# Start-up loads, early stores and the next-memory copy of a recurrent attention kernel re-planned together

## The chip, the cores and the metric

The kernel runs on one core of a Trainium2 chip. The metric is the device time of one execution in microseconds (us), taken over several runs; the profile shows one execution and its span, which is some 1.8 us shorter than the time of the same run. The engines are PE (TensorE, matmuls; "PEld" are its weight loads), DVE (VectorE), ACT (ScalarE), POOL (GpSimd) and SP (SyncE, which only issues transfers).

## The reference

Two layers of recurrent attention with a small memory, each followed by a dense layer, every one on the layernorm of its input and added to it:

```python
for s in range(n_seg):                       # 2048 rows in 64 segments of 32, one after the other
    h = concatenate([mem, x[s]])             # 8 rows of memory + 32 rows, 512 columns
    q, k, v = h @ Wq, h @ Wk, h @ Wv         # 32 heads of 128
    p = softmax(where(mask, q @ k.T * scale, -1e9))
    o = (p @ v) @ Wo                         # back to 512 columns
    mem = o[:8]                              # the next segment needs it
    out.append(o[8:])
...
x = x + A(layernorm(x)); x = x + B(layernorm(x))     # B: 512 -> 1376 -> relu -> 512
x = x + A(layernorm(x)); x = x + B(layernorm(x))     # the same weights again
```

The memory chains the 64 segments. What a segment needs of `x` alone (values, layernorm) can be done ahead; what it needs of `mem` can't.

## The kernel before

The two attention layers are interleaved, the second one four segments behind, which gives 68 steps (0 to 67). The kernel does not write its instructions in a fixed order. It first describes all operations to a planner, each with its engine, its estimated cost and the keys that it reads and writes; the planner simulates the engines, picks by priority among the operations that are ready, and the operations are then issued in the planned order. The priorities are tables of numbers found by search, one entry for a kind of operation and a phase of the run (step 0 and step 2 have a phase each, steps 1 and 3 share one, the even and the odd middle steps have one each, and so have the even and the odd last steps):

```python
RULE = (0.0714, 334.5336, ...)      # look-ahead, bonus for staying in the column mode, ...
PERIOD = 40.244
PLACE = {("attend.mmu0.0", 0): 609.348, ("attend.mmu0.0", 1): -183.486, ... }   # PE operations
PAIRED = { ... }                    # matmul groups that may be cut into 64-column halves
AHEAD = { ... }                     # operations of the other engines

            if PE in o.cost:
                o.prio = PERIOD * o.step + PLACE.get((o.key, phase(o.step)), 0.0)
            ...
                # a rule of the planner's model, not a measurement: a block of 64 matmuls
                # is planned to end no sooner than FETCH us after the block four before it
                for i in range(issued // BLOCK + 1, (issued + n) // BLOCK + 1):
                    t1 += max(0.0, blocks[-4] + FETCH - (t1 + ...))
```

The parts that the change touches:

```python
    # prepare(): the first loads, on ACT's queue
        plan.op(ACT, 0.45, get_x, w=[xb0])             # x rows of group 0
        plan.op(ACT, 0.45, get_memory, w=[mb0])
    ...
    # prepare_group(g): x rows of groups 1 to 7, also on ACT's queue
            plan.op(*((ACT, 0.45) if early else (SP, 0.78)), load, r=[*gate, *(rows if g > 1 else [])], ...)
    ...
    # project(k): once the output of step k is in the PSUM bank st, its memory rows go to HT,
    # which the queries and keys of step k+1 read
            def ev():
                nc.vector.tensor_copy(out=HTn[:, :, m_lo:m_hi], in_=v(2 * W)[:, :, m_lo:m_hi])

            plan.op(DVE, 0.15, ev, r=[wo], w=[("HTm", i), ("taken", k)])
    ...
    # main loop: POOL writes the early groups' x and values back to HBM (early_stores), SP then loads
    # the dense weights into the room that those values held (load_dense)
            if k in (1, 2):
                while stores:
                    early_stores([("sc", 1, 0)])       # behind the first scores of step 1
                load_dense(k, u)
```

Of the kernel before, what the change touches and what calls it, by code (L numbers as in the profile page):

```python
# [28 lines left out]
BLOCK, FETCH = 64, 7.0  # L29

RULE = (0.0714, 334.5336, 21842.5159, 2217302446.7678)
PERIOD = 40.244
PLACE = {
    ("attend.mmu0.0", 0): 609.348, ("attend.mmu0.0", 1): -183.486, ("attend.mmu0.0", 2): 147.437,
    ("attend.mmu0.0", 3): -78.515, ("attend.mmu0.0", 4): 65.61, ("attend.mmu0.0", 5): 366.858,
    ("attend.mmu0.0", 6): -249.718, ("attend.mmu1.0", 0): 726.903, ("attend.mmu1.0", 1): 684.118,
    ("attend.mmu1.0", 2): -19.8, ("attend.mmu1.0", 3): 132.658, ("attend.mmu1.0", 4): 129.759,
    ("attend.mmu1.0", 5): 371.411, ("attend.mmu1.0", 6): -353.4, ("attend.mmu2.0", 0): -14.873,
    ("attend.mmu2.0", 1): -1055.665, ("attend.mmu2.0", 2): 375.184, ("attend.mmu2.0", 3): 495.749,
    ("attend.mmu2.0", 4): 267.365, ("attend.mmu2.0", 5): 143.496, ("attend.mmu2.0", 6): -164.881,  # L40
    ("attend.mmu3.0", 0): 55.83, ("attend.mmu3.0", 1): 304.958, ("attend.mmu3.0", 2): -27.575,
    ("attend.mmu3.0", 3): 521.565, ("attend.mmu3.0", 4): -53.654, ("attend.mmu3.0", 5): -33.75,
    ("attend.mmu3.0", 6): 139.713, ("attend.mmu4.0", 0): -1004.936, ("attend.mmu4.0", 1): -1157.418,
    ("attend.mmu4.0", 2): -270.186, ("attend.mmu4.0", 3): -964.038, ("attend.mmu4.0", 4): -328.51,
    ("attend.mmu4.0", 5): 58.406, ("attend.mmu4.0", 6): -138.434, ("dense_layer.mm.0", 1): 844.726,
    ("dense_layer.mm.0", 3): 771.51, ("dense_layer.mm.0", 6): 794.222, ("dense_layer.mm.1", 1): 595.059,
    ("dense_layer.mm.1", 3): 282.976, ("dense_layer.mm.1", 6): -365.611, ("dense_layer.mm.2", 1): 402.759,
    ("dense_layer.mm.2", 3): 201.475, ("dense_layer.mm.2", 6): 383.89, ("dense_layer.mm.3", 1): 375.463,
    ("dense_layer.mm.3", 3): 375.816, ("dense_layer.mm.3", 6): 544.49, ("dense_layer.mm.4", 1): -1179.846,
    ("dense_layer.mm.4", 3): -271.405, ("dense_layer.mm.4", 6): -220.579, ("dense_layer.mm.5", 1): 907.374,  # L50
    ("dense_layer.mm.5", 3): 373.845, ("dense_layer.mm.5", 6): 565.451, ("finish_pair.turn.0", 1): -90.833,
    ("finish_pair.turn.0", 3): -375.688, ("finish_pair.turn.0", 6): -738.706, ("g0", 2): -581.803,
    ("g1", 2): -1043.701, ("g2", 2): 282.751, ("g3", 2): -205.545, ("g4", 2): 584.676, ("g5", 2): -60.649,
    ("g6", 2): 371.668, ("g7", 2): 288.938, ("late_values.mmv0.0", 0): -64.904, ("late_values.mmv1.0", 0): 678.294,
    ("late_values.mmv2.0", 0): 101.482, ("late_values.mmv3.0", 0): 44.512, ("late_values.mmv4.0", 0): 351.071,
    ("late_values.mmv5.0", 0): -24.294, ("late_values.mmv6.0", 0): -120.477, ("late_values.mmv7.0", 0): -996.402,
    ("layernorm.turn.0", 1): 92.873, ("layernorm.turn.0", 3): -23.204, ("layernorm.turn.0", 6): 193.698,
    ("layernorm.turn.1", 1): 910.291, ("layernorm.turn.1", 3): -857.558, ("layernorm.turnr.0", 0): -337.322,
    ("layernorm.turnr.1", 0): -831.277, ("prepare.turns.0", 2): 390.358, ("project.mm.0", 0): 359.615,
    ("project.mm.0", 1): -869.571, ("project.mm.0", 2): -60.568, ("project.mm.0", 3): -169.635,  # L60
    ("project.mm.0", 4): 156.569, ("project.mm.0", 5): 430.997, ("project.mm.0", 6): -293.953,
    ("project.mm.1", 0): 824.231, ("project.mm.1", 1): 252.725, ("project.mm.1", 2): 43.429,
    ("project.mm.1", 3): 540.792, ("project.mm.1", 4): -164.609, ("project.mm.1", 5): 588.5,
    ("project.mm.1", 6): 101.76, ("project.mm.2", 0): 126.782, ("project.mm.2", 1): -862.581,
    ("project.mm.2", 2): -235.851, ("project.mm.2", 3): 70.544, ("project.mm.2", 4): -259.138,
    ("project.mm.2", 5): -117.671, ("project.mm.2", 6): -300.67, ("project.mm.3", 0): 223.614,
    ("project.mm.3", 1): -213.188, ("project.mm.3", 2): -93.552, ("project.mm.3", 3): 545.141,
    ("project.mm.3", 4): 351.716, ("project.mm.3", 5): -238.608, ("project.mm.3", 6): -107.853,
    ("project.mm.4", 0): 230.883, ("project.mm.4", 1): -148.91, ("project.mm.4", 2): -568.124,
    ("project.mm.4", 3): 379.873, ("project.mm.4", 4): -132.884, ("project.mm.4", 5): 770.552,  # L70
    ("project.mm.4", 6): 66.643, ("queries_keys.mmu0.0", 0): -119.1, ("queries_keys.mmu0.0", 1): -850.808,
    ("queries_keys.mmu0.0", 2): -204.722, ("queries_keys.mmu0.0", 3): -113.926, ("queries_keys.mmu0.0", 4): 59.817,
    ("queries_keys.mmu0.0", 5): -235.287, ("queries_keys.mmu0.0", 6): -320.902,
    ("queries_keys.mmu0.1", 0): -402.058, ("queries_keys.mmu0.1", 1): 10.017, ("queries_keys.mmu0.1", 2): 261.017,
    ("queries_keys.mmu0.1", 3): -213.134, ("queries_keys.mmu0.1", 4): -297.361, ("queries_keys.mmu0.1", 5): -84.629,
    ("queries_keys.mmu0.1", 6): -888.993, ("queries_keys.mmu0.2", 0): -392.541,
    ("queries_keys.mmu0.2", 1): -333.397, ("queries_keys.mmu0.2", 2): -356.282, ("queries_keys.mmu0.2", 3): -51.387,
    ("queries_keys.mmu0.2", 4): -331.518, ("queries_keys.mmu0.2", 5): -853.492,
    ("queries_keys.mmu0.2", 6): -1044.343, ("queries_keys.mmu0.3", 0): -40.65, ("queries_keys.mmu0.3", 1): -57.543,
    ("queries_keys.mmu0.3", 2): -41.34, ("queries_keys.mmu0.3", 3): -1060.763, ("queries_keys.mmu0.3", 4): -376.858,  # L80
    ("queries_keys.mmu0.3", 5): -120.052, ("queries_keys.mmu0.3", 6): -111.195,
    ("queries_keys.mmu1.0", 0): -259.357, ("queries_keys.mmu1.0", 1): -373.272, ("queries_keys.mmu1.0", 2): 371.489,
    ("queries_keys.mmu1.0", 3): -1015.198, ("queries_keys.mmu1.0", 4): 169.449,
    ("queries_keys.mmu1.0", 5): -376.609, ("queries_keys.mmu1.0", 6): -35.359, ("queries_keys.mmu1.1", 0): -890.304,
    ("queries_keys.mmu1.1", 1): -52.862, ("queries_keys.mmu1.1", 2): 261.214, ("queries_keys.mmu1.1", 3): -931.873,
    ("queries_keys.mmu1.1", 4): -80.004, ("queries_keys.mmu1.1", 5): -905.415, ("queries_keys.mmu1.1", 6): -75.569,
    ("queries_keys.mmu1.2", 0): -1032.537, ("queries_keys.mmu1.2", 1): -941.562,
    ("queries_keys.mmu1.2", 2): -245.647, ("queries_keys.mmu1.2", 3): -738.459, ("queries_keys.mmu1.2", 4): 282.479,
    ("queries_keys.mmu1.2", 5): -47.448, ("queries_keys.mmu1.2", 6): -355.274, ("queries_keys.mmu1.3", 0): -1042.76,
    ("queries_keys.mmu1.3", 1): -311.787, ("queries_keys.mmu1.3", 2): -329.768,  # L90
    ("queries_keys.mmu1.3", 3): -856.085, ("queries_keys.mmu1.3", 4): -47.655, ("queries_keys.mmu1.3", 5): -394.586,
    ("queries_keys.mmu1.3", 6): -257.527, ("queries_keys.mmu2.0", 0): -51.901, ("queries_keys.mmu2.0", 1): -283.405,
    ("queries_keys.mmu2.0", 2): -257.559, ("queries_keys.mmu2.0", 3): 302.184, ("queries_keys.mmu2.0", 4): 98.406,
    ("queries_keys.mmu2.0", 5): 305.605, ("queries_keys.mmu2.0", 6): 363.104, ("queries_keys.mmu2.1", 0): -34.459,
    ("queries_keys.mmu2.1", 1): 44.98, ("queries_keys.mmu2.1", 2): 334.384, ("queries_keys.mmu2.1", 3): -1093.708,
    ("queries_keys.mmu2.1", 4): -293.392, ("queries_keys.mmu2.1", 5): 351.704,
    ("queries_keys.mmu2.1", 6): -1178.673, ("queries_keys.mmu2.2", 0): -41.303, ("queries_keys.mmu2.2", 1): 58.94,
    ("queries_keys.mmu2.2", 2): 291.775, ("queries_keys.mmu2.2", 3): 52.266, ("queries_keys.mmu2.2", 4): -151.786,
    ("queries_keys.mmu2.2", 5): 228.689, ("queries_keys.mmu2.2", 6): 405.936, ("queries_keys.mmu2.3", 0): 330.979,
    ("queries_keys.mmu2.3", 1): 57.914, ("queries_keys.mmu2.3", 2): -40.37, ("queries_keys.mmu2.3", 3): 87.416,  # L100
# [1234 lines left out]
```

## Time and profile before

| | before |
|---|---|
| time, median (lowest to highest) | 1631.96 us (1631.00 to 1634.06), 4 runs beside the changed kernel; 1632.44, 3 runs, known at the prediction |
| span of the profiled run | 1630.9 us |
| PE, ACT, DVE busy | 97%, 66%, 64% |
| PE matmuls, priced at the trace's issue spacing | 1531.8 us |
| first Wv matmul | 12.72 us |
| next-memory copy of step 0, 4, 64, 66 | 56.64, 138.28, 1564.35, 1600.04 us |
| middle steps, even and odd (medians of steps 5 to 63) | 25.33, 22.15 us |

### The profile page before, as it was taken

The page shows a single profiled execution, that of the slowest core. Times are in us where ns is not written, and L with a number is a line of the kernel's source. Part 1 is how long each engine was busy: PE and PEld are TensorE (multiplying, and loading weights), DVE is VectorE, ACT ScalarE, POOL GpSimd, SP SyncE. Part 2 cuts the span into 40 slices and gives each one's busy share as a digit, 9 for nine tenths or more (in the row PEclk, how much of TensorE's full clock was granted, in tenths as well). Part 3 has the DMA queues.
Part 4 walks back from the last instruction along what each step waited for, and adds up shares of the span by engine and source line. Part 5 has one row for each costly group of instructions (what it writes and reads, how often), then busy time and mean ns, then how long its engine had stood idle before and what let it go on. Part 6 is the DMA issues. An engine that isn't in the chain of part 4 may idle for free.

```text
span 1630.9 us, 94544 instructions
## 1 busy us (share of the span) xinstructions
PE 1587.0 (97%) x43116; PEld 1380.4 (85%) x43179; DVE 1046.2 (64%) x3025; ACT 1079.6 (66%) x2717; POOL 139.9 (9%) x363
## 2 busy tenths in 40 slices
PE   7999999999999999999999999999999999999997
PEld 4778888888888888888888888888888888888886
DVE  4556766766665666676567567656656765665664
ACT  4556766766666676666667666666766666676664
POOL 4210000001000000100000010000000000000000
PEclk9999999999999999999999999999999999999999
DMA  9521001111100111111011011101101000000000
GB/s 370 199 85 36 18 23 27 25 26 35 34 21 22 29 25 25 35 29 25 23 29 25 25 35 28 25 23 29 25 26 26 25 19 19 19 20 19 16 6 6
DMA packets 42880, 63.30 MB, mean 39 GB/s; under 512 B 15400, under 2 KB 28816, under 8 KB 42480
## 3 DMA queue, kind: packets, MB, share of 16 engines
q1 hardware_dynamic: 35984, 35.88, 9.0%
q0 software_dynamic: 5328, 20.32, 3.3%
q8 instruction: 338, 5.54, 1.4%
q10 hardware_dynamic: 1168, 1.06, 0.2%
q14 instruction: 62, 0.51, 0.1%
HBM read 33.50 MB, written 11.93 MB: 28 GB/s over the span
## 4 chain that ended last, share of the span: by engine, by line
PE 93%; DVE 4%; issue 1%; ACT 1%; DMA 0%; POOL 0%; DVEq 0%; POOLq 0%; ACTq 0%
PE work L667 38%; PE st L667 19%; PE fill L1000 16%; PE fill L667 12%; PE work L1168 4%; PE work L1084 3%; DVE sm L1109 1%; DVE es L1095 1%; DVE mx L1099 1%; DVE P L1126 0%; DVE HT L1212 0%; DVE es L1102 0%; PE fill L791 0%; DMA xb<-in_A_x_dram 0%; ACT OT L921 0%
## 5 line engine op out<-in xcount | busy, mean ns | idle before, releaser
L667 PE MATMUL work<-HT,Wk_sb 128*128 128x80 bf16 (+2 forms) x10144 | 363.6, 200 | 9.7 <-DVE HT L1212 9.2
L667 PE MATMUL work<-HT,Wq_sb 128*128 128x80 bf16 (+2 forms) x9728 | 361.5, 200 | 0.4 <-DVE HT L1212 0.2
L667 PEld LDWEIGHTS <-Wk_sb 128*128 128x128 bf16 (+1 forms) x10144 | 330.8, 103 | 29.7 <-DVE HT L1212 12.8
L667 PE MATMUL st<-OT,Wo_sb 128*128 128x80 bf16 (+1 forms) x8704 | 339.7, 199 | 3.8 <-issue 1.8
L667 PEld LDWEIGHTS <-Wq_sb 128*128 128x128 bf16 (+1 forms) x9728 | 326.9, 102 | 13.5 <-DVE HT L1212 5.1
L667 PEld LDWEIGHTS <-Wo_sb 128*128 128x128 bf16 x8704 | 319.2, 99 | 13.1 <-issue 6.1
L1000 PE MATMUL fill<-Wv_sb,HT 128*64 128x512 bf16 x2176 | 273.5, 382 | 0.0
L921 ACT CAST kT<-work 128x320 bf16<-128x320 f32 (+1 forms) x537 | 219.8, 410 | 71.4 <-PE work L667 35.3
L921 ACT CAST qT<-work 128x320 bf16<-128x320 f32 (+1 forms) x484 | 197.8, 409 | 102.5 <-PE work L667 58.4
L1149 ACT ACTIVATE PT<-work,half 128x160 bf16<-128x160 f32 (+2 forms) x447 | 203.0, 469 | 18.0 <-DVE PT L1151 14.0
L921 ACT CAST OT<-work 128x320 bf16<-128x320 f32 (+1 forms) x387 | 149.6, 415 | 98.0 <-PE work L1168 97.9
L921 ACT CAST vw<-fill 128x512 bf16<-128x512 f32 x229 | 134.2, 586 | 104.2 <-PE fill L1000 102.1
L1095 DVE TENSOR_TENSOR es<-work,maskb 128x320 f32<-128x320 f32 (+2 forms) x340 | 130.5, 400 | 84.4 <-PE work L1084 81.6
L1000 PEld LDWEIGHTS <-HT 128*64 128x64 bf16 x2176 | 107.2, 110 | 72.5 <-issue 1.9
L1106 ACT ACTIVATE es<-es 128x320 f32<-128x320 f32 (+2 forms) x340 | 133.2, 406 | 8.3 <-DVE es L1102 3.5
L1126 DVE TENSOR_TENSOR P<-es,sm 128x320 bf16<-128x320 f32 (+2 forms) x337 | 131.2, 406 | 4.4
L1151 DVE TENSOR_SCALAR PT<-work,half 128x320 bf16<-128x320 f32 (+2 forms) x233 | 105.0, 454 | 44.8 <-PE work L667 42.7
L1102 DVE TENSOR_TENSOR es<-es,mx 128x320 f32<-128x320 f32 (+2 forms) x340 | 131.5, 403 | 1.5
L1099 DVE TENSOR_REDUCE mx<-es 128x8 f32<-128x320 f32 (+2 forms) x340 | 129.5, 397 | 2.8
L1109 DVE TENSOR_REDUCE sm<-es 128x8 f32<-128x320 f32 (+2 forms) x340 | 128.5, 394 | 1.6 <-ACT es L1106 1.5
L1212 DVE CAST HT<-st 128x64 bf16<-128x64 f32 (+1 forms) x67 | 14.8, 221 | 163.3 <-PE st L667 163.0
L1168 PE MATMUL work<-PT,vw 128*64 128x80 bf16 (+1 forms) x1384 | 106.1, 202 | 1.8 <-DVE PT L1151 1.7
(99 smaller groups left out, 1729.6 us busy)
## 6 DMA issues: line engine op xcount, KB each, us to landing
V<-vw SPq DMA_DIRECT2D x240, 48.0 KB
V<-vh SPq DMA_DIRECT2D x120, 64.0 KB
Wq_sb<-in_A_Wq_dram POOLq DMA_DIRECT2D x2, 2048.0 KB, 20.7
Wk_sb<-in_A_Wk_dram POOLq DMA_DIRECT2D x2, 2048.0 KB, 25.0
Wo_sb<-in_A_Wo_dram POOLq DMA_DIRECT2D x2, 2048.0 KB, 36.1
vh<-vg SPq DMA_DIRECT2D x32, 128.0 KB
Wv_sb<-in_A_Wv_dram POOLq DMA_DIRECT2D x1, 2048.0 KB, 12.1
vh<-w_sb POOLq DMA_DIRECT2D x4, 512.0 KB, 7.2
```

The lines of the kernel that those rows point to most:

```text
L667: nc.tensor.matmul(out_[u:v, :], lhsT=lhsT[:, u:v], rhs=rhs, start=start, stop=stop, tile_position=(0, u), **more)
L921: nc.scalar.copy(out=out_, in_=in_)
L1000: nc.tensor.matmul(vp[64 * b:64 * b + 64, :], lhsT=cols(c4), rhs=Wv_sb[:, c4, n * 512:(n + 1) * 512], start=(c4 == 0), stop=(c4 == NC4 - 1 ...
L1095: nc.vector.tensor_tensor(out=flat(es[:, A]), in0=flat(sp[:, A]), op=ALU.add, in1=maskb[:, a_lo:a_hi, :].unsqueeze(2).to_broadcast([128, n ...
L1099: nc.vector.tensor_reduce(out=mx[:, As], in_=es3(), axis=AX.X, op=ALU.max)
L1102: nc.vector.tensor_tensor(out=es3(), in0=es3(), op=ALU.subtract, in1=mx[:, As].unsqueeze(2).to_broadcast([128, ns * na, L]))
L1106: nc.scalar.activation(out=es[:, A], in_=es[:, A], func=ACTF.Exp, scale=SCALE)
L1109: nc.vector.tensor_reduce(out=sm[:, As], in_=es3(), axis=AX.X, op=ALU.add)
L1126: (nc.gpsimd if eng == POOL else nc.vector).tensor_tensor(out=o, in0=flat(es[:, A]), op=ALU.mult, in1=sm[:, As].rearrange("p (a s) -> p a ...
L1149: nc.scalar.activation(out=o, in_=i, func=ACTF.Copy, scale=half[:, b:b + 1])
L1151: nc.vector.tensor_scalar_mul(out=o, in0=i, scalar1=half[:, b:b + 1])
L1168: nc.tensor.matmul(o[u:u + cols, :, a, :], lhsT=V[:, p, e0 + u:e0 + u + cols], rhs=PT[:, a, 2 * i + h2, :, :], start=True, stop=True, tile ...
```

## The change

The intent: PE is starved at the start, so bring x of group 0 in first, get the early stores and dense weights out of the way right behind the last attention weights, let whichever engine is free copy the next memory, and find the priorities again for the new plan. The hunks that are not tables:

```diff
-BLOCK, FETCH = 64, 7.0
+BLOCK, FETCH, LOADED = 64, 7.0, (75.0, 9.5)        # 9.5 in place of FETCH up to 75 us of planned time
-RULE = (0.0714, 334.5336, 21842.5159, 2217302446.7678)
-PERIOD = 40.244
+RULE = (0.0676, 338.0438, 3554579.0286, 1242705613.0663)
+PERIOD = 42.8582
 ... PLACE, PAIRED, AHEAD: every number new ...
-                    t1 += max(0.0, blocks[-4] + FETCH - (...))
+                    t1 += max(0.0, blocks[-4] + (FETCH if t > LOADED[0] else LOADED[1]) - (...))

-        plan.op(ACT, 0.45, get_x, w=[xb0])
-        plan.op(ACT, 0.45, get_memory, w=[mb0])
+        plan.op(ACT, 0.45, get_x, w=[xb0, "x0"])
+        plan.op(ACT, 0.45, get_memory, r=["x0"], w=[mb0, "start"])
 ...
-  ... load, r=[*gate, *(rows if g > 1 else [])],
+  ... load, r=[*gate, *(["start"] if early else []), *(rows if g > 1 else [])],

-            def ev():
-                nc.vector.tensor_copy(out=HTn[:, :, m_lo:m_hi], in_=v(2 * W)[:, :, m_lo:m_hi])
-            plan.op(DVE, 0.15, ev, r=[wo], w=[("HTm", i), ("taken", k)])
+            def ev(eng):
+                copy_on(eng, HTn[:, :, m_lo:m_hi], v(2 * W)[:, :, m_lo:m_hi])
+            copy_op(64, ev, r=[wo], w=[("HTm", i), ("taken", k)], more={ACT: 0.01, DVE: 0.02})

             if k in (1, 2):
-                while stores:
-                    early_stores([("sc", 1, 0)])
                 load_dense(k, u)
 ...
         project(k, act, seg)
+        while stores:
+            early_stores([("taken", 0)])               # behind the next-memory copy of step 0
```

## The prediction

> **What bounds the kernel now.** I read the page first, then the busy time by stretch, then the timeline of TensorE (PE) at both ends and in one middle step, then its waits.
>
> ```profile
> PE 1587.0 (97%) x43116; PEld 1380.4 (85%) x43179; DVE 1046.2 (64%) x3025; ACT 1079.6 (66%) x2717; POOL 139.9 (9%) x363
> PEclk9999999999999999999999999999999999999999
> q8 instruction: 338, 5.54, 1.4%
> ```
>
> PE is busy 97% of 1630.9 us at full granted clock; no other engine passes 66%. So the change can only win PE's idle 44 us, or make PE do less. The stretches say where the idle time lies (columns: us; busy and instructions of PE, PEld, DVE, ACT, POOL; clock, DMA share, GB/s):
>
> ```profile
> 0.00:40.00 40.00, 27.86 (x374) 17.17 (x375) 17.14 (x47) 19.60 (x39) 15.81 (x39) 1.00 0.96 370
> 40.00:80.00 40.00, 39.09 (x1044) 30.19 (x1041) 22.22 (x86) 23.61 (x73) 11.00 (x23) 1.00 0.56 200
> 80.00:120.00 40.00, 36.81 (x1040) 30.91 (x1036) 24.04 (x91) 23.98 (x78) 5.84 (x15) 1.00 0.32 96
> 600.00:900.00 300.00, 297.34 (x8106) 260.92 (x8117) 200.23 (x564) 205.48 (x506) 22.43 (x60) 1.00 0.11 27
> 1600.00:1631.00 31.00, 21.66 (x561) 17.94 (x560) 14.06 (x51) 11.88 (x38) 0.79 (x2) 0.87 0.03 7
> ```
>
> Idle are 12.1 us in the first 40, 3.2 us in 80 to 120, 2.7 us in a middle stretch of 300, and 9.3 us in the last 31. The tail (layernorm, dense layer and store of the last rows) is a chain that the change does not touch. What it aims at is the first 120 us. PE's own timeline there:
>
> ```profile
> 9.29 0.61 PE L667 MATMUL fill<-ident,xr 128*128 128x128 bf16 x4 [2.01 <-DVE xr L718]
> 11.44 0.61 PE L667 MATMUL fill<-ident,xr 128*128 128x128 bf16 x4 [1.54 <-DVE xr L718]
> 12.72 3.63 PE L1000 MATMUL fill<-Wv_sb,xg 128*64 128x512 bf16 x16 [0.68 <-ACT xg L921]
> ...
> 44.12 0.73 PE L667 MATMUL work<-HT,Wk_sb 128*128 128x40 bf16 x23 [0.47 <-issue]
> ...
> 89.58 0.20 PE L667 MATMUL st<-OT,Wo_sb 128*128 128x40 bf16 x2 [1.41 <-issue]
> ```
>
> PE starts real work at 12.72 us. "<-issue" means that nothing the profile shows held it. I counted PE's instructions in program order: the six such pauses (44.12, 50.86, 82.84, 89.58, 93.59, 97.59 us) come before instructions 960, 1216, 3008, 3264, 3520, 3776, all 192 past a multiple of 256. So PE waits for its next block of instructions; they sum to 2.9 us. Where DMA is nearly full (0.97 to 1.03 busy at 40 to 50 and 80 to 90 us) two such pauses end 6.74 us apart; at 90 to 100 (0.08) 4.0 us apart.
>
> [...] the first 16 Wv matmuls take 213 ns each (12.72 to 16.13), later ones 108; but it lasts until 19 us. The granted clock row doesn't show it. [...] the trace issues 16 in 0.574 us, 35.9 each. [...] 338 packets x 256 = 86,528 against 86,360 PE instructions[...] VectorE (DVE) sits idle 163 us ahead of the 64 next-memory copies.
>
> **The change part by part.** The instruction orders of both programs were compared; most of the diff is priorities for the order, found again.
>
> Amount of work. Counted by shape and priced at this trace's issue spacing (35.9 ns for 128x80, 18 for its 64-column half, 108 for 64x512, and so on), PE's matmuls sum to 1531.8 us before and 1531.9 after. The 567 extra matmuls are whole ones cut in halves (Wq: 480 fewer of 35.9 ns, 960 more of 18): 0 us. Switches between 64- and 128-column mode cost about 0.09 us (812.42 to 812.52); 309 become 303: -0.5 us (eight fewer in the last three steps, two more at the start).
>
> x of group 0 first. Now the order on ScalarE's (ACT's) queue is group 1, group 0, memory, and x0 lands 5.6 us after issue (1.25 to 6.87). Group 0 will be issued at 0.79 and group 1 about 1 us later than now. DVE can't begin on x0 before 5.2 us (it fills banks until 5.19). From there by this trace's durations: statistics 0.7 and 0.2, power 0.9, normalise 0.4, transpose 0.6: group 0 turned at about 8.0 instead of 9.9. But the new PE order still puts group 1's transpose ahead of the first Wv matmul. Its power now queues behind three weight issues of 0.8 on GpSimd (7.0 + 2.4 + 0.8 = 10.2), normalise and transpose 1.1: 11.3 to 11.4 us against 12.72. **-1.3 us**.
>
> Early stores and dense weights. Today GpSimd stalls 12.7 us (54.3 to 67.0) and the stores and dense weights use DMA at 70 to 90 us, with 1.77 us of PE idle in 80 to 90. DMA is free at 60 to 70 (0.01 busy). The 7 stores of 640 KB and 2.8 MB of weights, 7.3 MB, at some 380 GB/s take 19 us: they move to about 50 to 70. That removes the 89.58 and 82.84 pauses, and some of the waits behind. Steps 1 to 4, by the spacing of their next-memory copies (17.9, 19.9, 18.5, 25.4 us) less their matmul work (16.9, 15.8, 15.7, 23.1), lose 10.1 us; 8 mode switches each (0.7) and 0.3 of handover would be 4. Of the 6 us excess I give 3 back: **-3 us**. Against it: PE wants a block of 256 every 4.6 us in 50 to 70 (526 matmuls in 20 us)[...]. Some pauses move there: **+1 us**, and part of the early start may be eaten at instruction 960 in the same way.
>
> Next memory on either engine. All 67 copies go from DVE to ACT. A DVE copy of 128x64 takes 225 ns; ACT takes 266 for 128 columns and 292 for 160, so about 215 for 64 (an estimate). The matmuls that fit between the last st matmul and the first that needs the copy are the same in the steady steps (649 ns in one step, none in the next), so 36 steps stay exposed: 36 x 10 ns, **-0.4 us**.
>
> Middle. Matmul work between step ends is identical step by step (24.44 and 21.43 us). The last 7 odd two-sided steps lose 1.5 us each against 0.7 before them, to softmax and OT waits; the new order starts scores there sooner. I give **-1 us**.
>
> Sum: -0.5 -1.3 -3 +1 -0.4 -1 = -5.2 us, so 1632.4 becomes about 1627.
>
> **Rivals.** (1) *Instruction fetch becomes the startup's limit.* For: the pauses at 44.12 and 50.86 already sit at full DMA, and the change keeps DMA full until 70. At 6.7 us a block, four blocks take 27 us instead of 19; a few us are lost at 50 to 70, the rest caught up at 4.0 a block. Against: the new order's matmul work per block differs by at most 1.6 us, and the two blocks before 960 came without pause. Time: 1630 to 1635. (2) *The transfers were hidden anyway.* For: only 1.8 us of PE idle in the busy stretch 80 to 90. Then only start, switches and tail count: about 1630. (3) *ACT becomes the wait.* It is at 66% and takes on waits of 2.5 us in each of 64 steps; but it already waits 97 us in 58 of them for the copy by DVE, and DVE gets its 163 us back. If queries and keys came late, each step would lose 0.1 us: 1634. (4) *The new order also clears the waits of steps 1 to 4 and the late steps*: 1621.
>
> **Range and chances.** Most terms are 1 to 3 us, so the range is these rivals' span: 1621 to 1633, centre 1627. 2% is 33 us, more than all reducible idle time (12 of the start, most of which has to stay, 4 behind it, 17 in the middle): faster 1%, slower 1%, same 98%.
>
> **What would show it.** First Wv matmul near 11.4 us; x0 landed by 5; stores at 46 to 60 and DMA idle after 70 us; no pause over 1 us near 89, perhaps new ones "<-issue" at 50 to 70 at 192 past a multiple of 256; next-memory copies on ACT of 200 to 225 ns with handover unchanged; 24.44 + 0.9 and 21.43 + 0.7 us middle steps as before; tail unchanged to 0.5 us. The prediction is wrong if middle steps change by over 0.1 us each (64 of them make 6 us), or if the fetch pauses at 50 to 70 sum to over 4 us.

What "lasts until 19 us" is the longer time of the first Wv matmuls (16 in 3.63 us from 12.72, 16 in 3.08 from 16.13, 16 in 1.92 from 19.89), 35.9 ns is the issue spacing of 128x80, and the 338 packets are those of the page's instruction queue (5.54 MB). That a pause is PE's wait for a block of 256 instructions is the author's reading of these counts and of the six places. The +1 us is the author's estimate. So is, in rival (3), that ACT would stand still at each copy; the trace shows only that DVE sat idle for 163 us ahead of 64 of them and ACT for 97 us behind 58.

## More of the kernel before

The start of the next-memory copy (from the bank `st` to `HT`) is a good ruler: there is one per step, it ends each step's chain, and both kernels have it. Where two kernels' copies drift apart, time was won or lost there.

The prediction shows the page, the stretches and the start of PE's timeline. It leaves out the end. There PE waits twice for DVE's part of a softmax, PT, once in step 65 and once behind the last copy; both times it has just transposed P and goes straight on to the product with PT (columns: start us, duration us, engine, line, operation, tiles, count; in brackets the idle time before it and what ended it):

```profile
1578.11 0.27 PE L667 MATMUL work<-ident,P 128*128 128x80 bf16 x3
1579.24 0.38 PE L1168 MATMUL work<-PT,vw 128*128 128x80 bf16 x6 [0.86 <-DVE PT L1151]
...
1614.71 0.38 PE L1168 MATMUL work<-PT,vw 128*128 128x80 bf16 x6 [0.87 <-DVE PT L1151]
```

## The result, and the profile after

| | before | after |
|---|---|---|
| time, median (lowest to highest) of 4 runs | 1631.96 us (1631.00 to 1634.06) | 1626.26 us (1625.63 to 1630.13) |
| span of the profiled run | 1630.9 us | 1624.3 us |
| first Wv matmul | 12.72 us | 11.75 us |
| next-memory copy of step 0, 4, 64, 66 | 56.64, 138.28, 1564.35, 1600.04 | 54.53, 136.28, 1560.43, 1595.02 |
| middle steps, even and odd | 25.33, 22.15 us | 25.32, 22.13 us |

The ratio is 0.9968, with a 95% interval of 0.9950 to 0.9987. (A ratio is the mean time of one kernel's runs over that of the other's of the same rounds, so not quite the ratio of the medians above.) The change is within 2%, faster by about 0.3%.

The page of the kernel after, two of the rows that the prediction quoted of the kernel before:

```profile
PE 1584.0 (98%) x43678; PEld 1378.5 (85%) x43746; DVE 1031.9 (64%) x2930; ACT 1095.1 (67%) x2813; POOL 139.2 (9%) x362
q8 instruction: 342, 5.60, 1.4%
```

PE is the same bound, 3 us less busy in a span that is 6.6 us shorter; ACT took some 15 us of work from DVE. The instruction queue moved four packets more (342, before 338), as 567 matmuls are cut in halves. The stretches of the kernel after (us; busy time and instructions of PE, PEld, DVE, ACT, POOL; clock, DMA share, GB/s):

```profile
0.00:40.00 40.00, 28.71 (x458) 18.50 (x459) 19.78 (x58) 21.12 (x46) 17.39 (x42) 1.00 0.97 372
40.00:80.00 40.00, 37.10 (x930) 27.69 (x928) 17.73 (x70) 22.29 (x67) 8.23 (x18) 1.00 0.79 273
80.00:120.00 40.00, 38.83 (x1178) 33.31 (x1174) 26.86 (x96) 25.49 (x82) 5.91 (x15) 1.00 0.09 21
600.00:900.00 300.00, 297.50 (x8218) 261.30 (x8230) 195.55 (x541) 207.62 (x521) 22.65 (x60) 1.00 0.11 27
1600.00:1624.30 24.30, 15.72 (x402) 13.02 (x398) 12.43 (x47) 8.78 (x30) 0.79 (x2) 0.89 0.02 5
```

Read against the prediction's rows: the transfers moved from the stretch 80 to 120 (DMA share 0.32, now 0.09) into 40 to 80 (0.56, now 0.79). PE lost 2.0 us there (39.09 to 37.10) and won 2.0 (36.81 to 38.83) later: a plain trade. The first 40 us gained 0.85 us of PE time. The middle is as it was. PE's timeline at the start, after:

```profile
10.67 0.61 PE L665 MATMUL fill<-ident,xr 128*128 128x128 bf16 x4 [2.40 <-DVE xr L716]
11.75 1.92 PE L998 MATMUL fill<-Wv_sb,HT 128*64 128x512 bf16 x8 [0.47 <-POOL HT L938]
...
41.59 0.58 PE L665 MATMUL work<-HT,Wk_sb 128*128 128x40 bf16 x17 [0.90 <-issue]
48.33 0.28 PE L665 MATMUL st<-OT,Wo_sb 128*128 128x40 bf16 x5 [0.72 <-issue]
75.41 0.81 PE L665 MATMUL work<-HT,Wk_sb 128*128 128x40 bf16 x26 [0.60 <-issue]
```

The first Wv matmul comes 0.97 us earlier. Where before had six pauses "<-issue" in the first 100 us, three are left, in front of instructions 960, 1216 and 2496, all 192 past a multiple of 256. They sum to 2.2 us where they were 2.9. The two at 960 and 1216, which before had too, grew from 0.6 to 1.6 us in sum. And at the end, the place of the two waits for PT shown above, here in step 65:

```profile
1573.14 0.96 PE L665 MATMUL st<-OT,Wo_sb 128*128 128x40 bf16 x32
1573.95 0.28 PE L665 MATMUL fill<-ident,xr 128*128 128x64 bf16 x4
1574.17 0.38 PE L1166 MATMUL work<-PT,vw 128*128 128x80 bf16 x6
1574.79 0.21 PE L665 MATMUL work<-ident,P 128*128 128x80 bf16 x1 [0.25 <-DVE P L1124]
```

The same six matmuls have no wait in front of them: between the transposes of P (at 1573.03) and the product PE now does 32 `st` matmuls, which take 0.8 us, and transposes a block of `xr`, 0.2 us, and by then PT is there. Behind the last copy 32 `st` matmuls (at 1607.63) fill most of the wait. The copy itself, by engine (line, engine, operation, tiles, forms, count; busy us, mean ns; idle before, releaser), in the kernel before and then in the kernel after:

```profile
L1212 DVE CAST HT<-st 128x64 bf16<-128x64 f32 (+1 forms) x67 | 14.8, 221 | 163.3 <-PE st L667 163.0
```

```profile
L919 ACT CAST HT<-st 128x64 bf16<-128x64 f32 (+1 forms) x67 | 14.0, 209 | 84.6 <-PE st L665 83.5
```

All 67 copies went to ACT, where one takes 12 ns less on average (the 60 of 128x64 alone: 212 ns, 225 on DVE). That DVE's 163 us of idle time vanished from this row bought nothing by itself: DVE is not the bound.

With the ruler of the copies, after minus before (us):

```
step       0      1      2      3      4      20     40     50     64     65     66     end
after    -2.11  -0.29  -0.49  -1.71  -2.00  -2.00  -2.38  -3.38  -3.92  -5.06  -5.02  -6.60
```

(PE's new order does 0.87 us less matmul work before the copy of step 0 and makes it good in step 1, so the first column flatters.) Three places gain: the start 2.0 us up to step 4, the middle 1.9 us in 60 steps, the end 2.7 us, of which 1.1 in step 65 and 1.6 after the last copy.

### The profile page after: what moved, and what is told of

It is laid out like the page before. It is cut to its first block, busy times and chain, and to the rows that moved or that the text cites. A ratio compares the mean times of both kernels' runs of the same rounds, so it can differ in the third digit from the quotient of the medians.

```text
span 1624.3 us, 95837 instructions
## 1 busy us (share of the span) xinstructions
PE 1584.0 (98%) x43678; PEld 1378.5 (85%) x43746; DVE 1031.9 (64%) x2930; ACT 1095.1 (67%) x2813; POOL 139.2 (9%) x362
## 4 chain that ended last, share of the span: by engine, by line
PE 94%; DVE 3%; issue 1%; ACT 1%; POOL 0%; DMA 0%; DVEq 0%; POOLq 0%; ACTq 0%
PE work L665 39%; PE st L665 19%; PE fill L998 15%; PE fill L665 12%; PE work L1166 4%; PE work L1082 3%; DVE es L1093 0%; DMA hT<-in_A_x_dram 0%; DVE mx L1097 0%; ACT HT L919 0%; PE fill L789 0%; DVE sm L1107 0%; DVE vw L921 0%; DVE PT L1149 0%; DVE es L1100 0%
## 5 line engine op out<-in xcount | busy, mean ns | idle before, releaser
L665 PE MATMUL work<-HT,Wq_sb 128*128 128x80 bf16 (+2 forms) x10208 | 369.3, 200 | 8.2 <-ACT HT L919 8.1
L665 PE MATMUL work<-HT,Wk_sb 128*128 128x80 bf16 (+2 forms) x10144 | 368.2, 200 | 2.4 <-issue 1.5
L665 PEld LDWEIGHTS <-Wq_sb 128*128 128x128 bf16 (+1 forms) x10208 | 330.4, 103 | 25.8 <-ACT HT L919 11.6
L1147 ACT ACTIVATE PT<-work,half 128x320 bf16<-128x320 f32 (+2 forms) x448 | 200.6, 467 | 31.5 <-PE work L665 15.0
L884 DVE TENSOR_TENSOR xg<-xg,fill 128x512 f32<-128x512 f32 (+1 forms) x34 | 23.4, 688 | 185.9 <-PE fill L665 185.9
L800 DVE TENSOR_TENSOR xg<-xg,fill 64x512 f32<-64x512 f32 x30 | 20.4, 681 | 140.5 <-PE fill L665 140.5
## 6 DMA issues: line engine op xcount, KB each, us to landing
Wv_sb<-in_A_Wv_dram POOLq DMA_DIRECT2D x1, 2048.0 KB, 11.4
```

The costliest lines, as they stand in the source:

```text
L665: nc.tensor.matmul(out_[u:v, :], lhsT=lhsT[:, u:v], rhs=rhs, start=start, stop=stop, tile_position=(0, u), **more)
L1147: nc.scalar.activation(out=o, in_=i, func=ACTF.Copy, scale=half[:, b:b + 1])
```

## The experiments

The reasons to be told apart. **Theory A**: the parts do little by themselves, the new order found for them all does the work. **Theory B**: each part wins where it acts (x first at the start, the stores and weights at 80 to 90 us, the copy in every step). Further, two rivals at the start: pauses at instruction blocks, and the half rate of PE's first Wv matmuls (213 ns each in before, 108 later). What the tables fix are priorities, not the order itself: the planner simulates anew for every kernel, so a changed load rule changes PE's order as well. Of the kernels below, the copy alone has PE's order of before, and copy back, stores back and stores held have that of after; x first alone, new priorities alone, x not first and all parts with the old priorities have orders that belong to neither. Twelve kernels ran, all correct. "Before" is the kernel before on the same chip, 9 runs (medians 1631.15 to 1632.04).

### x of group 0 first, alone

```diff
 (the kernel before)
-        plan.op(ACT, 0.45, get_x, w=[xb0])
-        plan.op(ACT, 0.45, get_memory, w=[mb0])
+        plan.op(ACT, 0.45, get_x, w=[xb0, "x0"])
+        plan.op(ACT, 0.45, get_memory, r=["x0"], w=[mb0, "start"])
   and "start" among what the early x loads read
```

> The kernel before plus only the new order of the first loads (x of group 0, memory, then the later groups), old priorities. Theory A (the parts of the change act each by itself): first Wv matmul about 1 us earlier than 12.72 (11.75 in the full change), span 1 to 2 us under 1630.9. Theory B (instruction blocks set the pace of the first 60 us): the start is earlier, but the pauses at instructions 960 and 1216 grow and the copy of step 1's next memory comes within 0.5 us of 74.54, span within 1 us of 1630.9.

Measured: 1633.39 us, ratio 1.0012 (1.0000 to 1.0025). The first Wv matmul came at 11.37 instead of 12.72 us and the copy of step 2 was 3.4 us ahead; at step 3 the lead was down to 0.45, and it stayed near that. PE's order changed with the rule, from 19 us on. The largest pause of this run comes in step 3:

```profile
93.49 0.83 PE L667 MATMUL work<-HT,Wk_sb 128*128 128x40 bf16 x27 [1.92 <-issue]
```

This is instruction 3520, a block border (as the places 192 past a multiple of 256 are called here), behind ten us of full DMA (share 1.00 at 80 to 90). In before the pauses there came a step earlier and summed to 2.0 us in step 2, so half of the 3.4 us is only that PE has not paused yet: the lead at the copies of steps 0 and 1 was 1.7 us, and 0.4 at step 4. That the old place of the stores and weights took the difference fits the pause, but is not shown: from 80 us on the pauses of before sum to 2.2 us, those of this run to 1.9.

### The copy on either engine, alone

```diff
 (the kernel before)
-            def ev(): nc.vector.tensor_copy(...);   plan.op(DVE, 0.15, ev, ...)
+            def ev(eng): copy_on(eng, ...);         copy_op(64, ev, ..., more={ACT: 0.01, DVE: 0.02})
```

> The kernel before plus only the next-memory copy on either engine; the build puts all 67 on ACT and leaves the order on PE as it was. Theory A: each of the some 30 exposed handovers is 0.02 us or less shorter (212 ns on ACT against 225 on DVE in the two profiles), -0.4 to -1.3 us in all. Rival: ACT, which now waits for st, delays the queries and keys behind it, and the span grows by 1 us or more.

Measured: 1631.80 us, ratio 1.0005 (0.9991 to 1.0019). PE's order stayed that of before. The even middle steps took 25.32 us instead of 25.33 (0.016 us less), the odd ones 22.15 as before: 0.5 us over the run, below what single steps scatter.

### The new priorities alone, and all parts with the old priorities

```diff
 (new priorities alone: the kernel after without its three parts)
   RULE, PERIOD, PLACE, PAIRED, AHEAD and LOADED of after; loads, stores and copy of before

 (all parts, old priorities: the kernel before with them)
   loads, stores, copy and LOADED of after; RULE, PERIOD, PLACE, PAIRED, AHEAD of before
```

> The kernel after with its three code changes (x first, early stores, copy on either engine) taken back, so the new priorities alone. Theory A: most of the gain of the middle's sporadic steps (26, 50, 53: -1.3 us) and of steps 65 and 66 (-1.7 us) is here, and the start is as before: span 1626 to 1628. Rival (the gain is in the code changes): within 1 us of 1630.9.

> The kernel before with all code changes of the diff, but the old priorities. Theory A: start 1 us earlier and handovers 0.02 us shorter, none of the gains of the late and last steps: span 1628 to 1630. Rival (the priorities were tuned to the old code and do harm with the new): 1632 or more.

Measured: the new priorities alone 1633.01 us, ratio 1.0013 (1.0000 to 1.0025); all parts with the old priorities 1637.62 us, ratio 1.0038 (1.0025 to 1.0051), the slowest kernel. So neither half of the change gains: **of what ran, only the parts and the priorities found for them together do.** Two limits: `LOADED` alone, with the old tables, changes PE's order too (built, not run), and with the old tables the store rule changes no instruction, so in the second kernel the transfers stay late (DMA share 0.03 at 60 to 70 us, 0.94 at 80 to 90). And no priorities were searched again for the old parts, so whether a new search would have gained without them stays open. Both lose at the start, 5.2 and 4.1 us by step 4. First PE's timeline and two stretches of the run with the new priorities alone:

```profile
62.95 0.28 PE L665 MATMUL work<-HT,Wk_sb 128*128 128x40 bf16 x5 [1.81 <-issue]
```

```profile
62.00:64.00 2.00, 1.05 (x33) 0.91 (x34) 0.05 (x1) 0.58 (x2) 0.00 (x0) 1.00 0.03 10
64.00:66.00 2.00, 2.00 (x14) 0.90 (x12) 0.92 (x3) 0.81 (x2) 0.00 (x0) 0.53 0.00 0
```

then those of the run with all parts and the old priorities:

```profile
89.48 0.30 PE L1168 MATMUL work<-PT,V 128*128 128x80 bf16 x4 [1.20 <-issue]
95.95 0.89 PE L667 MATMUL work<-HT,Wk_sb 128*128 128x40 bf16 x27 [1.71 <-issue]
```

```profile
90.00:100.00 10.00, 7.59 (x251) 7.41 (x251) 0.81 (x4) 3.68 (x14) 0.00 (x0) 0.83 0.50 156
```

The pauses stand at instructions 1728, 3264 and 3520, all 192 past a multiple of 256; the first run has one more of 1.58 us at 85.63 (instruction 2752). They come where transfers are dense or have just been (DMA share 0.99 at 58 to 60, 0.94 at 80 to 90); that an order searched for these transfers would avoid them is not shown. In both runs PE's granted clock was then lower, 0.53 over two us in the one (64 to 66; PE had been busy for 2.20 of the four us before) and 0.83 over ten in the other (90 to 100), so in these two the pauses were not all that was lost. The length of the pause alone does not decide it: with the pause of 2.32 us below, the clock was 1.00 from 60 to 80 us.

But the end is won by the priorities alone: with them, the copy of step 65 comes 16.45 us after that of step 64, in before 17.60.

### The kernel after with one part taken out

```diff
 (copy back on VectorE)                    (x of group 0 not first)
-            copy_op(64, ev, ...)          -  get_x w=[xb0, "x0"], get_memory r=["x0"] w=[.., "start"]
+            plan.op(DVE, 0.15, ev, ...)   +  get_x w=[xb0], get_memory w=[mb0]

 (early stores back in their old place)
             if k in (1, 2):
+                while stores:
+                    early_stores([("sc", 1, 0)])
                 load_dense(k, u)
```

> The kernel after with the next-memory copy put back on DVE; the order on PE stays the same. Theory A: 60 middle steps lose 0.02 us each again, so the copy of step 64 comes 1.2 us later than in the kernel after, the copy of step 4 within 0.3 us of it; span 1625.5. Rival (the copy on ACT also frees DVE and so carries the gain of the start or of the tail): the difference is over 2 us, or sits in steps 0 to 4 or 65.

> The kernel after without the rule that the later groups' x loads wait for group 0; new priorities, early stores and copy on ACT kept. Its order on PE is that of the run with the new priorities alone, which was 5.2 us later at step 4 than the kernel before. Theory A (the new priorities fit only the early start): again some 7 us later than the kernel after at step 4, and span 1630 to 1632. Rival (the early stores or the copy made the start): within 2 us of the kernel after.

> The kernel after, with the early stores put back in their old place in the plan. Statically the orders on TensorE, VectorE and ScalarE are those of after; on GpSimd one store changes places with one copy, on SyncE a weight issue with an x issue. If the early stores come early because of the priorities that were found again (theory A), this run is the kernel after within 0.1%: a span of 1623 to 1626 us, x stores and dense weights at 54 to 73 us. If the moved rule itself is worth the predicted 3 us, it is at 1627 or more.

Measured: without the copy on ACT 1629.27 us, ratio 0.9984 (0.9972 to 0.9997); without x first 1634.61 us, ratio 1.0015 (1.0001 to 1.0028); without the moved store rule 1628.04 us, ratio 0.9975 (0.9962 to 0.9987), against 0.9968 of the kernel after.

Taking out x first costs all of the gain and more. PE then runs another order, the one of the new priorities alone, and its timeline has the longest pause:

```profile
63.97 0.28 PE L665 MATMUL work<-HT,Wk_sb 128*128 128x40 bf16 x5 [2.32 <-issue]
```

The store rule, a named part of the change, does next to nothing in the kernel after. On the old priorities it builds the very same program as before, instruction for instruction on all five engines (this needed no run). In the kernel after, undoing it swaps one store with one copy on POOL and the place of one weight issue on SP, and leaves PE, DVE and ACT untouched. There the stores come early because their priorities do. It does act where x is not first. The kernels with the new priorities alone and with x not first have the same order on PE, and this rule is all that parts their orders on POOL and SP (built with the rule undone, the second has those of the first). POOL's last four early stores come at 73.2 to 74.8 us without the rule and at 57.5 to 60.0 with it. The copy of step 4 is then 2.7 us earlier, with the copy on ACT as well, but the two ratios, 1.0013 and 1.0015, are alike.

What the run without the rule gives, in the kernel after, is thus nearly a repeat of that kernel, and shows the scatter. Its PE timeline:

```profile
42.61 0.58 PE L665 MATMUL work<-HT,Wk_sb 128*128 128x40 bf16 x17 [1.09 <-issue]
49.35 0.28 PE L665 MATMUL st<-OT,Wo_sb 128*128 128x40 bf16 x5 [0.72 <-issue]
80.64 0.84 PE L998 MATMUL fill<-Wv_sb,HT 128*64 128x512 bf16 x6 [1.28 <-issue]
```

The first two pauses stand in front of the same groups as after; the third came one block later (instruction 2752 instead of 2496) and twice as long. At step 4 this run was 0.77 us ahead of before, the kernel after 2.00. With the copy on DVE it was 0.68, so that run's loss is mostly this scatter too; its even middle steps are back at 25.33. The expected span of 1623 to 1626 us was missed by the profiled run (1628.0), which was the slowest of its five (1625.0 to 1628.0).

A part of the scatter of the start can be seen. PE runs the first Wv matmuls at half rate (in after the first 8 start 214 ns apart, the 16 from 18.32 us on 108), and how long that lasts differs though PE's order is the same. The second group of Wv matmuls, in the kernel after and then with the copy on DVE:

```profile
13.46 2.43 PE L998 MATMUL fill<-Wv_sb,xg 128*64 128x512 bf16 x16
13.45 3.41 PE L998 MATMUL fill<-Wv_sb,xg 128*64 128x512 bf16 x16
```

It took 3.01 us with the stores back. The copy of step 0 goes the same way: 54.53 us after a group of 2.43, 55.55 after 3.01, 55.80 after 3.41.

### The stores held back in the kernel after

```diff
 (the kernel after, at the issue of the planned order)
+        held, n = [], 0
         for o in plan.order():
+            if n < 4 and (o.eng == POOL and o.kind.endswith("put") or held and o.eng == SP):
+                held.append(o); continue
             emit(o)
+            if o.eng == POOL and o.kind == "prep_x.cp":
+                n += 1
+                if n == 4:                     # at about 70 us
+                    for h in held: emit(h)
```

> The kernel after with the stores of all 7 groups, and the loads that follow them, held back until GpSimd has made step 3's copy (about 70 us), where the kernel before had them; PE, ACT and DVE keep their order. Theory B (instruction blocks are fetched slowly while DMA is full): no pauses beyond 0.1 us in 50 to 70, and pauses over 1 us in sum in 75 to 95, all 192 past a multiple of 256 instructions; the copy of step 1 comes about 0.8 us earlier, those of steps 2 and 3 1 to 3 us later; span 1625 to 1628. Rival (transfers are hidden wherever they lie): the copies of steps 1 to 4 move by less than 0.4 us.

Measured: 1633.65 us, ratio 1.0012 (0.9996 to 1.0027). PE, DVE and ACT keep the order of after; only POOL's stores and what SP issues behind them come later. The start is as after up to the copy of step 1 (0.8 us better); then the timeline of PE, and two stretches:

```profile
78.84 0.84 PE L998 MATMUL fill<-Wv_sb,HT 128*64 128x512 bf16 x6 [1.02 <-issue]
82.91 0.29 PE L665 MATMUL fill<-ident,xr 128*128 128x64 bf16 x4 [0.95 <-DVE xr L716]
86.14 0.50 PE L665 MATMUL work<-HT,Wk_sb 128*128 128x40 bf16 x14 [0.85 <-issue]
89.74 0.63 PE L665 MATMUL fill<-xnM,w_sb 128*64 128x64 bf16 x28 [0.92 <-DMA w_sb<-in_B_w_dram]
92.33 1.52 PE L665 MATMUL fill<-xnM,w_sb 128*64 128x64 bf16 x33 [1.55 <-issue]
```

```profile
92.00:94.00 2.00, 1.67 (x43) 1.60 (x43) 0.03 (x1) 0.68 (x3) 0.00 (x0) 0.63 0.92 262
94.00:96.00 2.00, 2.00 (x42) 1.77 (x40) 1.08 (x4) 0.76 (x3) 0.00 (x0) 0.52 0.06 21
```

Three block pauses, two waits for what was late, and a granted clock of 0.63 and 0.52 behind them (92 to 96 us): the copy of step 2 came 5.5 us later than in after, more than the 1 to 3 expected, because the waits and the clock add to the pauses. So with this order on PE the early place of the transfers is worth some 7 us (ratio 1.0012 against 0.9968), even though the kernel after, with them early, gained only 2.0 us at the start against before, whose priorities go with the late place.

### Warm, shifted, and one whole block ahead

```diff
 (the kernel after; into the unused bank st, from a tile of zeros)
+        def warm(n):
+            for _ in range(n):
+                nc.tensor.matmul(b_st.tiles[0][:, 0:C], lhsT=Pt[2][:, 0:128], rhs=Pt[2][:, 0:C], start=True, stop=True)
   warm:   C = 512, 18 at 1.3 us and 9 behind the memory transposes  (54 instructions)
   shift:  C = 8,   27 at 1.3 us                                     (54 instructions)
   block:  C = 80,  96 and 32 in the same two places                 (256 instructions)
```

> The kernel after with 27 matmuls that nothing reads, 18 from 1.3 us on and 9 behind the memory transposes, in PE's idle time. [...] the Wv matmuls from 11.75 us on take 108 ns each from the first (213 now until about 14.7) and PE is 1.5 us ahead at 15 us. Theory B: the pauses move 54 instructions earlier in the program but keep their count of instructions (960, 1216), arrive within 0.5 us of 41.6 and 48.3, grow by about what was won, and the copy of step 0 gains less than 0.7 us; span 1623.8 to 1624.6. Rival (the pauses have another cause, tied to the matmuls they precede): they stay ahead of the same matmuls, and the 1.5 us are kept: span 1622.8.

> The kernel after with 27 matmuls of 8 columns ahead of all others (54 more instructions[...]). It parts the two things that the warm run did at once. If a later place of the block borders won the start there, this run shows pauses near 47 and 77 us, as the warm run, and a span near 1623.3. If warm TensorE did, the first 8 Wv matmuls still take 1.9 us and the span is near 1624.3 or more. In both cases pauses are to sit at instructions 192 past a multiple of 256 of this program: 1216 inside the st matmuls, 2752 inside the Wq matmuls.

> The kernel after with 128 matmuls of 80 columns (256 instructions, one block) in the idle time ahead of the first Wv matmul: warm as in the warm run, but every block border falls where it falls in after, one block later in the count. If borders decide where TensorE pauses, the pauses are back in front of the same groups as in after (Wk x17 near 41, st x5 near 48, Wk x26 near 75), minus any that the warm start made due at another time; the first 8 Wv matmuls take about 1.05 us. Span 1623 to 1625 us. If one more block at full DMA makes TensorE wait for blocks earlier, a pause shows before 35 us and the span is 1625 to 1627.

Measured: warm 1625.71 us, ratio 0.9962 (0.9950 to 0.9975), the best median, though not told apart from the kernel after; shift 1626.59 us, ratio 0.9962 (0.9948 to 0.9975); block 1627.62 us, ratio 0.9971 (0.9958 to 0.9983). PE's timelines, of the warm run,

```profile
11.75 1.05 PE L998 MATMUL fill<-Wv_sb,HT 128*64 128x512 bf16 x8 [0.68 <-POOL HT L938]
18.15 1.92 PE L998 MATMUL fill<-Wv_sb,HT 128*64 128x512 bf16 x16 [0.65 <-ACT w_sb L919]
46.99 0.96 PE L665 MATMUL st<-OT,Wo_sb 128*128 128x40 bf16 x32 [0.29 <-issue]
77.32 0.78 PE L665 MATMUL work<-HT,Wq_sb 128*128 128x40 bf16 x25 [0.61 <-issue]
```

of the shifted run,

```profile
11.75 1.92 PE L998 MATMUL fill<-Wv_sb,HT 128*64 128x512 bf16 x8 [0.47 <-POOL HT L938]
47.50 0.96 PE L665 MATMUL st<-OT,Wo_sb 128*128 128x40 bf16 x32 [0.24 <-issue]
78.08 0.78 PE L665 MATMUL work<-HT,Wq_sb 128*128 128x40 bf16 x25 [1.08 <-issue]
```

and of the run with a whole block ahead:

```profile
16.57 1.92 PE L998 MATMUL fill<-Wv_sb,xg 128*64 128x512 bf16 x16 [1.12 <-DMA Wv_sb<-in_A_Wv_dram]
41.38 0.58 PE L665 MATMUL work<-HT,Wk_sb 128*128 128x40 bf16 x17 [0.72 <-issue]
48.13 0.28 PE L665 MATMUL st<-OT,Wo_sb 128*128 128x40 bf16 x5 [0.72 <-issue]
78.40 0.84 PE L998 MATMUL fill<-Wv_sb,HT 128*64 128x512 bf16 x6 [0.50 <-issue]
```

This settles what the pauses are. With 54 instructions ahead, they leave their groups and appear in front of instructions 1216 and 2752 of the new count, warm or not. With exactly 256 ahead they are back in front of Wk x17 and st x5, as in after. They belong to a place in the instruction stream, not to the work there. Two pauses at neighbouring borders ended 6.74 us apart at a DMA share of 0.99 to 1.02 (before, 44.12 to 50.86 and 82.84 to 89.58; after, 41.59 to 48.33), 7.30 and 6.19 in the run with the stores held (78.84 to 92.33; share 1.02 at 80 to 90), and 4.0 at 0.22 and 0.02 (before, 89.58 to 97.59). Why a block comes late is not shown. The rival that one more block would add a pause before 35 us fell: none came.

On the half rate at the start it says less. Warm, the first eight Wv matmuls take 1.05 us instead of 1.92 (shifted they take 1.92 too: 27 matmuls of 8 columns did not change it), and then PE waits for ACT or for the Wv weights themselves (0.65 and 1.12 us above). The group of 40 Wv matmuls that all these kernels share starts at 31.88 us (warm), 32.38 (shift), 31.46 (block), 31.48 (after) and 32.32 (after without the store rule): of the half rate at the start at most 0.9 us is left by then, and the run's scatter is as large. Shifted without warmth gives the same ratio as warm; the spans of its five runs (1623.1 to 1625.3) surround the 1623.3 of the warm profile. At the copy of step 4 the two warm profiles are 3.2 and 2.7 us ahead of before, the four without warm-up that have the same order and early transfers 2.4, 2.0, 0.8 and 0.7: a gain of about 1 us at the start is possible, but these runs cannot tell it in the total.

### Only the last steps' priorities, in the kernel before

```diff
 (the kernel before)
   PLACE entries of phases 5 and 6 and AHEAD entries of part 2 (steps 64 to 67) from after; all else of before
```

> The kernel before with only the priorities of the last steps (phases 5 and 6 of the table, part 2 of the look-ahead) taken from after; the first steps, the copy on VectorE, the loads and the general rule stay. TensorE's first 5119 instructions are those of before; in the middle mostly names of banks change. If the gain of after at the end is the new order of the last steps by itself (theory A), the wait of 0.87 us for PT by VectorE is gone both in step 65 and behind the last copy: step 65 takes 16.5 us instead of 17.6, the stretch after the last copy some 30 instead of 30.9, the span is 1628 to 1629.5 and the ratio 0.9985 to 0.999. If it needs the other parts of the change (the general rule, the copy on ScalarE), step 65 stays at 17.6 and the span within 1630 to 1632.

Measured: 1630.62 us, ratio 0.9994 (0.9980 to 1.0008). PE's timeline of step 65 of this run:

```profile
1577.41 0.96 PE L667 MATMUL st<-OT,Wo_sb 128*128 128x40 bf16 x32
1578.22 0.28 PE L667 MATMUL fill<-ident,xr 128*128 128x64 bf16 x4
1578.44 0.38 PE L1168 MATMUL work<-PT,vw 128*128 128x80 bf16 x6
```

The wait is gone, here and behind the last copy; step 65 went from 17.60 to 16.51 us, and the stretch after the last copy from 30.86 to 30.44. The mechanism is shown and it needs none of the other parts. The time is not: a gain of 1.5 us is 0.09%, less than this interval can tell, and this run lost 0.6 us at the start by scatter.

## Why the prediction was right or wrong

The total was right: 1627.0 predicted, 1626.26 measured, well inside the range. The mechanism, small terms at the start and no change of the bound, was right too. The terms by themselves were partly mis-sized, and some errors cancelled.

- **x of group 0 first, -1.3 us.** Nearly right. The first Wv matmul came 0.97 us earlier, at 11.75 instead of 11.3 to 11.4: it now reads `HT` and waits 0.47 us for POOL's copy into it, which the sum did not have. Freed of the work moved to step 1, the copy of step 0 gained 1.2 us. As the prediction said it might, the block at instruction 960 ate some: the pause there grew from 0.47 to 0.90 us. Alone, this part gained 1.35 us at the first Wv matmul, 1.7 at the copy of step 0, and kept 0.4 at step 4.
- **Early stores and dense weights, -3 us, and +1 us for pauses that move.** Right in direction, too large. Steps 1 to 4 brought 0.8 us net instead of 2. The prediction's step "the stores come at 46 to 60 and DMA is idle after 70 us" failed: POOL still stood 11.2 us before its second store of values, now for an eviction by ACT. The line of POOL's timeline:

```profile
53.70 0.55 POOL L961 DMA_DIRECT2D vh<-w_sb  x1 [11.17 <-ACT w_sb L919]
```

  So most stores came at 54 to 61, one at 69.7, the weights were issued at 59 to 73, and DMA was busy until some 76 us (share 0.84 at 73 to 76, 0.06 at 76 to 78). The long pause near 89 us went, as predicted; of the pauses feared at 50 to 70 none came, one of 0.6 us stood at 75. The rival "instruction fetch becomes the limit" was right in kind and too gloomy: the pauses at block borders sum to 2.2 us. A small slip in its sum: 526 matmuls in 20 us are a block every 4.9 us, not 4.6. And the step that gave the credit to the moved rule was wrong: in this kernel the rule moves one store, the found priorities move the others.
- **Next memory on either engine, -0.4 us.** Right in mechanism: 212 ns on ACT for 128x64, 200 to 225 predicted, 13 ns less than on DVE where 10 were expected. The even steps gain 0.016 us with it in all runs where ACT copies, so 0.5 us in all.
- **Middle, -1 us.** Taken with the copy, 1.4 us predicted and 1.9 seen in this pair of profiles. The repeatable part is smaller: 30 even steps by 0.016 and 30 odd ones by 0.02 us, 1.1 us. The -1 us was given to the waits of the last odd steps; these, 51 to 63, gained 0.4 us in sum, so that reading mostly failed. The rest is single steps that took 0.2 to 0.8 us longer in one run and not in another with the same order: steps 5 to 63 sum to 1404.2 us in after, 1405.8 in its near-repeat, 1404.9 in the shifted one, 1406.1 in before.
- **Mode switches, -0.5 us.** No run parts them from the rest; left open.
- **"Tail unchanged to 0.5 us."** This step failed, and is the largest error of size: the end gained 2.7 us. I had looked at the last dense chain, which indeed did not change (its wait of 3.27 us for `xr` is 3.27 after), and had not compared the softmax waits of steps 65 to 67, where the new order puts 32 `st` matmuls between the transposes of P and the product with PT. Step 65's 1.1 us appear in each of the nine runs with the tables of after, and in the run with only their last entries, and in none of before, x first, copy alone and all parts with the old priorities (17.60 to 17.63). After the last copy the nine runs with the tables of after take 29.9 us on average (29.3 to 30.4) and the four others 30.9 (30.5 to 31.2), so some 0.6 of the 1.6 us is this one run's luck.

The sum as it happened, in the pair of profiles: -2.0 at the start, -1.9 in the middle, -2.7 at the end, together -6.6. The sum as predicted: -3.3 at the start without the switches, -1.4 in the middle, nothing at the end, and -0.5 anywhere. A term that was too hopeful at the start was made good by an end that was not looked at. That the total came so close is in part luck. What stays open: how much of the start's 2.0 us repeats (with the same order on PE up to there, 0.7, 0.8 and 2.0 were seen, and the length of the half-rate phase goes with it), and why single middle steps take longer.

## What to carry to other kernels

The priorities here were found by search for one plan, and the parts of a later change could not be valued one by one: each piece alone here (x first, copy, all new priorities, those of the end) gave between a gain of 0.06% and a loss of 0.13%, hardly more than noise, all parts with the old priorities a loss of 0.38%, and only with the priorities found again a gain of 0.32%. Before crediting a rule, build the program with the rule alone and compare the instruction streams; a moved gate that yields the same stream explains nothing. When priorities are held and a rule is changed, compare the order of the main engine first: the planner may have made a third one. And compare the whole timeline, the end included, before writing "unchanged": a wait of 0.9 us that unrelated matmuls can fill is easily missed in a program that is 97% busy.
